# Another order of issue for the first 929 steps of a DeltaNet and MLP-mixer kernel

## The chip, the cores and the metric

The kernel runs on one core of one Trainium2 chip. The metric is the device time of one execution in microseconds, as the median of several runs. Besides TensorE (PE in the profile, with its weight loads as PEld) the core has VectorE (DVE), ScalarE (ACT), GpSimd (POOL) and SyncE (SP), which issues the DMA transfers. Each engine works through its own instructions in their order and waits on semaphores for the others.

## The reference

A linear recurrence of 8 heads with a 48 x 48 state each runs over 768 tokens for 4 batches. Its output, the heads side by side, goes through a token mixer and a channel mixer. Cut to what matters:

```python
B, H, S, D = 4, 8, 768, 48
k_n = k / (norm(k) + 1e-6)
for t in range(S):                       # per batch and head
    y[t] = q[t] @ state
    v_old = k_n[t] @ state
    state = state + beta[t] * outer(k_n[t], v[t] - v_old)
x = y.transpose(0, 2, 1, 3).reshape(B, S, H * D)          # [4, 768, 384]
h = relu(x.transpose(0, 2, 1) @ w_tok1) @ w_tok2          # 768 -> 256 -> 768
u = x + h.transpose(0, 2, 1)
out = u + relu(u @ w_ch1) @ w_ch2                         # 384 -> 1536 -> 384
```

## The kernel before

The recurrence is worked in chunks of 64 tokens. Two chunks make a unit u of 128 tokens, and a batch has 6 units, so there are 24 units and 48 chunks. For each chunk the products of the keys with one another are made, and with them a triangular system whose inverse turns the recurrence within the chunk into matrix products. The mixer follows batch by batch.

The work is written as generators, which stop after each step (a handful of instructions). They stand in a dictionary `jobs` under short names:

- `k3` loads the keys and queries of unit 3 (SP; copies on ACT, L396). `p3` prepares it: squares on ACT (L465), their sums on DVE (L468), the norm on ACT (L473, L474) and DVE (L477, L478), masks (L499), transposes on PE (L488, L507) with their copies on ACT (L491, L511), scaled keys (L516).
- `c3` and `d3` are the products of its two chunks (PE L442), with the masked evacuation on DVE (L445).
- `t3` takes the diagonal blocks out for the inversion (L598 on ACT, L603 on DVE, L605 on POOL). From the second round on they go through DRAM (L612 writes `n_dram`, L659 reads it into `x`).
- `i0`, `i1`, `i2` are rounds of that inversion, a chain of steps on DVE (L657, then pairs L676 and L680, then L682 to L693). `i0` serves the first units, `i1` and `i2` later ones. `f`, `h` and `j` join the inverted blocks into the inverse of a chunk (PE L710, L725, L760, L773; ACT L622, L716, L731, L754, L778; DVE L629, L749).
- `v3` loads values. `r10` is the recurrence's step for chunk 10: PE L837, ACT L843, PE L813, DVE L820, PE L851 and L852, DVE L860, ACT L865.
- `m0` is the mixer of batch 0: PE L1009, ACT L1017, PE L1022, six additions on DVE (L1026), transposes (PE L1032, ACT L1036), products (PE L1089 and later lines).
- `w29` is one piece of the weights: SP loads it (L273), ACT splits it (L279, L280), DVE shifts a part (L282), POOL joins the parts (L286). The load buffers are three, so a load waits for POOL's work on the piece three earlier. Some pieces of the last weight also make differences on DVE (L301). `s` sums weights, `b` loads beta.
- `x`, `z` and `Y` are products that nobody reads (L227, L237), which keep TensorE active.

Nothing reorders these steps. A string lists them, and a loop takes one step for each name (a number behind a star repeats it):

```python
    for word in order.split():
        name, _, n = word.partition("*")
        for _ in range(int(n or 1)):
            next(jobs[name])
```

The string has 2740 steps, and the order of instructions on each engine, the DMA issues on SP among them, follows from it. Buffers are counted: two for the values, two and two banks of PSUM for preparation and recurrence, three for the mixer.

Of the kernel before, what the change touches and what calls it, by code (L numbers as in the profile page):

```python
# [23 lines left out]
def kernel(  # L24
# [149 lines left out]
    t11 = const.tile([128, NB, HB], FP32, name="t11")  # L174
# [18 lines left out]
    w1 = const.tile([128, NCH, DTOK], FP32, name="w1")  # L193
    w2 = const.tile([128, NDH, S], FP32, name="w2")
# [993 lines left out]
    p1 c1*3 k2*4 p2 d1 x d1*3 k3 t0 p2*2 w3 d1 p2*2 w13 p2*4 c2*2 d2 p2 p3*2 k4*3  # L1188
    d2 k4*2 w3 w13 k6 w3*2 t0 w13*2 c2*2 k6 d2 k6 w1 k6*2 p3 k6 c2 d2*2 p3 x p3*5
    c3 d3 k4 c3 t1*2 p4 d3 x w18 c3 t1 t2 w18*2 w8 d3 c3 d3 k5 v1*2 d3 p4*2 k5*2 t0  # L1190
    c3 t2*2 t3*2 k7 p4 w1 t3 i0 p6 i0 p6*2 p4*2 i0*7 k8 z p4*4 v1 c4 k8 w6 d4 w1
    c4*4 d4*2 w8 w6 i0*2 d4 z v0*2 i0*3 x k8 z*3 w1 i0*2 d4 x w17*3 t4 z h0*4 i0
    k5*2 h1*2 k8 h1*2 h0 h1 w17 z f0*3 h0 w8*2 p3 v1 h0 p5 f1*3 k8 h0*3 v1 v0 h0*2
    v0 h2*3 t4 h2 h0 z f2 h2 w0*2 j0 w11 j0 w6 j0*4 k5 h1*6 j0*3 h1*2 f2*2 j1 p5 t4
    v0 j0*2 w6 p5*6 h2 p5 r0 w14 h2*2 r0*4 h2*4 c5*4 k7 k9 h2 r0*2 p8 p5 j1 c5 j1*2
    r0 k7 r1*2 k7 k9 r1 k9 w0*2 r1 d5*3 r1 k9 w11*3 d5*2 j1 r1 w14 p6*2 w9 p8 v2 j1
    h3*2 t5 j2 r1 p6 h3*2 f3 r1 k9*2 h3 j1*2 w14 j1*3 k7 p6 t5*2 r1*2 r2*3 w9 r2 x
    j2*3 i1*2 w14 j2*2 p6 r2*2 w16 r2 p6 f3*2 h3 i1*4 k10 r2*2 h3 i1 h3 d6 h3 p6 r2
    r3*2 d6 r3 d6 r3 i1 v2 x i1 h3*4 r3 d6 v2*2 w16 c6*2 w9 c6*2 k10 d6 c6 p7 w16
    p7 r3 j3 j2*2 r3 p7 r3*2 j2*2 j3 w9 j3 r4*2 k7 v3 p7 r4*2 j2 r3 j3*2 v2 j3 w16  # L1200
    r4 k10 p7*2 w24 v3 r4*2 k10 i1*2 t6 i1 w5 p7*2 r4 w27 p7 j3*4 r4*2 d7 i1 r5 i1
    r5 i1 r5 j3 k8 v3*2 d7 r5*2 d7*3 k10 w5 c7*3 r5 w27 w5 v4 r5 w5 c7*2 r5 p8*3
    r5*2 r6*4 w24 v4 t7 i1 z p8*4 p9 v3 r6 h5 w27 h5 v4*2 h5*3 r6*2 w26 h4*2 t7 d8
    h4 w24 i1 h4*2 t7 d8*3 r6 w24 w27 t7 c8*4 t6*2 f4*3 d8 h4*3 p9 w26 p9 r6 r7 k10
    r7 r6 h4 p8 c8 w28 t6 h4*3 v4 r7*2 h4 w7 p9 r7 p9*2 r7 p9*2 r7*2 p9 c9 w26 w28
    j4 d9 c9 w26 k11 c9*2 f5 p10 w28*2 d9*3 r7 c9 r8*2 w7 t8*2 d9 r8*2 j4*2 p10 t8
    j4*2 w7 j4 p7 p10 t8 v5 m0 f5 p10 p9 f5 v5 j4*3 w4 w15 w4 r7 t9*2 w4 j4*2 t9*2
    h5 w15 z r8*2 h5*2 v5 h5 v5 r8*2 w27 w7 w4 w15 Y r8 r9*4 h5*3 r8 p10 h5 i2 j5*2
    r9*2 i2 w29 j5 p10*2 r9 j5 i2*3 j5 w29 w12 k11*2 k12 j5 r9 i2 k11 v7 m0 r9 w15
    r10 j5*2 i2 j5 w12 w29 r10*2 i2 w19 i2 r10 p10 m0 p10 w19 k11*2 r9 v5 w12*2 k12  # L1210
    d10*2 i2 w22 j5 d10 j5 r10*2 x i2 d10 i2 r10 w19 Y r10 i2*2 m0 w29 r10 w19 z
    w21 Y p11 k12 r11 r10 w31 Y i2 w22*2 r11*3 k12 i2*2 r11 i2 m0 r11 i2*2 w22 v7*2
    c10 w31 r11*2 c10*2 i2 k12*2 r11 m0 x i2*4 v7 k12 i2*4 x z w25 v6*2 m0 i2*2 v6
    k12*2 v6 k12 i2 f6 m0*2 c10 m0 f6*3 w25 m0 c10 m0 w21 w25*3 f7 m0*2 p11 w21*2
    w23 f7 m0*2 w27 d10 m0 p11 j6 v6 j6*4 p10 f7 w31*2 f7 w30 f8*3 p12 j6 j7 p12
    w29 w23 t10 w29 w23 f9 m0 w25 j7 p12 j7*4 f8 m0 p11*3 r12*3 p12 r12 f9 r12 w23
    j8*2 f9 w30 t10 w23 r12 j8*3 r12*2 r13*3 j8 v7 w30 r13*2 m0 r13*2 p11 w32 p12
    p11*2 r13 t10 w20 s*2 k12 w30 w20 k12 v8 c11 w32 d11 c11 d11 r13 r14 t10 d11
    w31 r13 k13 c11 r14 w20 c11 w20 w23 d11 c11 d11 p12*2 r14*3 k13 m0*3 v8 w32 r14
    w32 k13*2 d12 c12*2 d12 c12 d12 c12*2 k13 w25 d12*2 p12 w31 r14*4 k13*2 m0*2  # L1220
    w27 w23 k13 r15*2 w29 k13*2 r15 j9 p11 p13 r15*2 p13 m0 p13*2 k13 p13 k13 p13
    r15 p13 m0*3 v8 w33 v8 d13 c13 t12 d13 c13 d13 c13 d13 c13 t11 r15*2 p13 r15
    t11*2 d13 c13 m0*2 t11 w33 r16*2 t12 r16 f9 t12 k14 r16 k14 j9*2 k14*2 w33*2 v8
    r16 j9*3 k14*2 m0*2 k14*2 m0 t13 m0 r15 t13 w33 r16 w33 p14*2 j9*2 t12 r16*3
    w33 r16 w31 m0 r17 p14*2 t13 j9 r17*2 j9 r17 p14 r17 t13 i3*2 k14 i3 m0*2 r17
    k14 v10 k15*2 i3*3 p14 i3 m0 k14 m0 i3 k14 v10 p14 i3*3 m0*2 i3 m0 k15*2 m0 r17
    i3 r17 m0 r17 v9*2 m0*2 i3*7 m0*3 i3*7 r18*2 i3*2 k15 v9 d14 r18 v9 k15*6 v10
    v9 i3*2 r17 i3 r18*2 f10 p15 m0*9 j9 f10*2 m0*2 f11 r18*2 k15 c14 d14 c14 d14
    p15 c14 d14 v10 r18 d14 r18 m0*4 r18 p15 r19 c14 s j10 r19*3 s r19 p15*2 f10
    m0*2 v10 f11 m0 r19*2 j10 f11*2 j10*2 f12 f13 r19*2 j10 j11 k16*2 p14 m0 k16  # L1230
    r20 k16 r20 k16*2 c14 t14 r20*2 p15 f12*2 j10 r20 j11 k16 j11*3 m0 k16 p15
    k16*2 r19 m0 j11 m0 r20 m0 s r20*2 d15*2 v11 p16 c15 r20 j12 d15 p16 c15 t14
    d15 c15 v11*2 r21 v11 c15*2 r21 p16 k16 r21*3 d15 t15 m0*2 r20 r21 p16*2 r21
    p16 m0 r21*2 j12*2 k16 j12 f13 k17 r21 j12*2 p16 r22*4 m0*2 p15 v11 r22*3 p16
    m0 k17*2 r22 k17*2 s*3 k17 r22*2 c16 d16 t15 c16 d16 f12 d16*3 c16 t15 r23 c16
# [72 lines left out]
```

## Time and profile before

| | us |
|---|---|
| median of three runs | 645.19 (644.68, 645.19, 655.08) |
| the profiled execution | 644.78 |
| its span in the trace | 643.0 |
| TensorE busy | 614.6 |
| VectorE busy | 446.1 |
| ScalarE busy | 259.8 |
| GpSimd busy | 108.9 |

The span is the time from the first to the last instruction that the trace shows; the execution is 1.78 us longer. The mean clock that TensorE was granted is 0.989 of full speed. A row of the trace's timeline gives the start and the duration in us, the engine, the line, the operation, output and input with partitions x elements, how many instructions of the kind follow one another, and in brackets how long the engine had been idle before and what ended that.

### The profile page before, as it was taken

Reading aid. Unit: us, or ns where it says so; the run is one execution under the profiler, and the core shown is the slowest. Engines: PE = TensorE matmul, PEld = TensorE weight load, DVE = VectorE, ACT = ScalarE, POOL = GpSimd, SP = SyncE. Lnnn points to the kernel's source line nnn. Section 1 sums busy time; section 2 is a strip of 40 time slices with the busy share of each in tenths; the row PEclk is TensorE's granted clock in tenths of the full one; section 3 lists DMA queues with packets and bytes.
Section 4 is the critical chain, followed back from the end, with each engine's and each line's share of the span. In section 5 each row is a group of like instructions: output and inputs, shape, how many; then the busy total and the mean of one; then the engine's idle time right before and its main releaser. Section 6 shows DMA issues by size and latency. Waiting matters only on the chain. (4 is left out here: it accounts for less than half of the span.)

```text
span 643.0 us, 21493 instructions
## 1 busy us (share of the span) xinstructions
PE 614.6 (96%) x9136; PEld 533.5 (83%) x9136; DVE 446.1 (69%) x1132; ACT 259.8 (40%) x631; POOL 108.9 (17%) x147
## 2 busy tenths in 40 slices
PE   8589899999999999999999999999999999999997
PEld 5358776678888988869899999769999987999997
DVE  4986877978789656988858997685726253373643
ACT  7759787436503332134523332234325140232240
POOL 2446264144200222021200010010020000000000
PEclk9989999999999999999979999999999999999999
DMA  9766667545543454343442222203010000000000
GB/s 192 165 131 156 147 149 199 151 116 131 100 112 76 75 112 107 75 106 70 96 99 68 58 78 44 66 11 53 4 42 4 25 3 0 25 1 25 1 26 25
DMA packets 135776, 50.27 MB, mean 78 GB/s; under 512 B 114656, under 2 KB 130144, under 8 KB 135680
## 3 DMA queue, kind: packets, MB, share of 16 engines
q1 hardware_dynamic: 135680, 48.89, 34.4%
q8 instruction: 72, 1.18, 0.8%
q14 instruction: 24, 0.20, 0.1%
HBM read 39.42 MB, written 9.44 MB: 76 GB/s over the span
## 5 line engine op out<-in xcount | busy, mean ns | idle before, releaser
L1111 PE MATMUL p_o<-wc,r 128*128 128x192 f32 x720 | 128.0, 332 | 0.6 <-ACT u_t L1036 0.6
L1111 PEld LDWEIGHTS p_o<-wc,r 128*128 128x128 f32 x720 | 118.5, 192 | 2.6 <-ACT u_t L1036 1.1
L993 DVE TENSOR_TENSOR r<-r,p_r 128x512 f32<-128x512 f32 x90 | 59.5, 683 | 39.4 <-PE p_r L981 36.9
L1040 DVE TENSOR_TENSOR xb<-xb,p_o 128x192 f32<-128x192 f32 x84 | 29.3, 350 | 57.5 <-PE p_o L1111 57.3
L990 ACT COPY r<-p_r 128x512 f32<-128x512 f32 x54 | 31.3, 584 | 85.9 <-PE p_r L981 78.6
L680 DVE TENSOR_TENSOR x<-x,sub 128x84 f32<-128x84 f32 (+24 forms) x178 | 59.9, 337 | 6.1
L676 DVE TENSOR_TENSOR sub<-x 128x84 f32<-128x84 f32 (+24 forms) x178 | 57.4, 322 | 6.5 <-DMA x<-n_dram 2.3
L1089 PE MATMUL p_c<-u_t,wc 128*128 128x256 f32 x216 | 51.3, 387 | 1.3 <-ACT r L1098 0.7
L1111 PE MATMUL p_o<-wc,s 128*128 128x192 f32 x288 | 51.2, 330 | 0.3 <-DVE xb L1040 0.3
L1111 PEld LDWEIGHTS p_o<-wc,s 128*128 128x128 f32 x288 | 46.8, 190 | 1.2 <-DVE xb L1040 0.6
L1089 PEld LDWEIGHTS p_c<-u_t,wc 128*128 128x128 f32 x216 | 39.6, 190 | 7.4 <-ACT r L1098 1.1
L416 POOL TENSOR_TENSOR v_st<-v_st,nrm 128x384 f32<-128x384 f32 x24 | 20.4, 849 | 148.1 <-DMA v_st<-in_v_dram 66.2
L442 PE MATMUL p_g<-kq 48*64 48x128 f32 (+1 forms) x704 | 38.6, 291 | 6.0 <-ACT kq L511 6.0
L997 ACT ACTIVATE r<-r 128x512 f32<-128x512 f32 x54 | 33.8, 631 | 25.5 <-DVE r L993 25.1
L499 POOL TENSOR_TENSOR mb<-mask_c,cs 128x512 f32<-128x512 f32 x20 | 21.0, 1049 | 129.6 <-DVE cs L478 103.7
L865 ACT ACTIVATE xb<-p_y 64x192 f32<-64x192 f32 x96 | 31.1, 324 | 24.0 <-PE p_y L852 16.3
L981 PE MATMUL p_r<-u_t,wc 128*128 128x128 f32 x288 | 38.6, 277 | 0.0
L981 PE MATMUL p_r<-t_d,wc 128*128 128x128 f32 x288 | 37.6, 281 | 0.0
L843 ACT COPY w_t<-p_w 128x192 f32<-128x192 f32 x48 | 15.3, 318 | 53.2 <-PE p_w L837 52.0
L442 PEld LDWEIGHTS p_g<-kq 48*64 48x64 f32 (+1 forms) x704 | 27.7, 140 | 10.0 <-ACT kq L511 6.8
L981 PEld LDWEIGHTS p_r<-u_t,wc 128*128 128x128 f32 x288 | 35.3, 192 | 0.3
L981 PEld LDWEIGHTS p_r<-t_d,wc 128*128 128x128 f32 x288 | 34.1, 191 | 0.9
(176 smaller groups left out, 1245.3 us busy)
## 6 DMA issues: line engine op xcount, KB each, us to landing
d<-in_moe_w_ch_dram SPq DMA_DIRECT2D x24, 384.0 KB, 3.9
v_st<-in_v_dram SPq DMA_DIRECT2D x96, 48.0 KB, 2.7
out_dram<-xb SPq DMA_DIRECT2D x23, 192.0 KB, 1.9
kst<-in_k_dram SPq DMA_DIRECT2D x64, 48.0 KB, 2.8
n_dram<-gm SPq DMA_DIRECT2D x72, 32.0 KB, 2.1
pads<-in_k_dram SPq DMA_DIRECT2D x24, 96.0 KB, 2.7
pads<-in_q_dram SPq DMA_DIRECT2D x24, 96.0 KB, 2.9
gm<-w_dram SPq DMA_DIRECT2D x72, 32.0 KB, 2.4
```

The lines of the kernel that those rows point to most:

```text
L442: nc.tensor.matmul(p_g[PAR[i ^ cc], p], kqt[f, p, cc, 0], kqt[f, p, cc])
L499: scaler.tensor_tensor(out=mb, in0=mask_c[:, None, None, :].to_broadcast([128, NP, 2, C]), in1=cs[:, :, :, None].to_broadcast([128, NP, 2, ...
L676: nc.vector.tensor_tensor(out=tmp, in0=col.to_broadcast(dims), in1=row.to_broadcast(dims), op=ALU.mult,)
L680: nc.vector.tensor_tensor(out=new, in0=new, in1=tmp, op=ALU.add)
L865: nc.scalar.mul(y[:, :, D * i : D * i + D], p_y[PAR[1 - i]], 1.0 if c else -1.0)
L981: nc.tensor.matmul(p[:, i], pieces[i // width][:, at : at + 128], f[f"u{n}"], start=first and i == 0, stop=True, skip_group_check=True,)
L990: nc.scalar.copy(o, p)
L993: nc.vector.tensor_tensor(out=o, in0=o, in1=p, op=ALU.add if sign > 0 else ALU.subtract)
L997: nc.scalar.activation(o, o, ACTF.Relu)
L1040: nc.vector.tensor_tensor(out=xb[:, c, e], in0=xb[:, c, e], in1=p, op=ALU.add)
L1089: nc.tensor.matmul(p_c[:, k], piece_of(wc1, cb, f * 128)[:, f * 128 : (f + 1) * 128], u_t[:, cb], start=(cb == 0), stop=(cb == NCB - 1),)
L1111: nc.tensor.matmul(p, a[:, m], wc2[:, m, j], start=(start and i == 0), stop=(i == NM - 1), skip_group_check=True,)
```

## The change

Only the string is different. Its first 929 steps are put in another order; every step that stood in the old string is there as often as before. The last 1811 steps are the same in the same order. The two strings begin like this:

```diff
     order = """
-    w10 z w10*2 z k1 z b k0 k1*2 b z x k1*2 k3 k0 z k1 k0*2 p1*2 k0 w2 k0 p0*2 b p1
-    p0 w10 p0*7 p1*3 k3*2 w2 d0 w2 c0 k2*2 c0 w18 d0*3 k3 w2 c0*3 d0 k3 p1*3 c1*2
...
+    z*4 w10*3 k1 k0 w10 b k0 k1*5 p1*2 k0*3 k3 k0 b p0 w2 p1 k2 b v1 p0*4 x k2 k3
+    p1 p0*2 p1 k4 p0 k3 p0 w2 k3 v1 w3 z c0 d0 c0 d0 k3 p0 d0 c0*2 k4 p1 w2*2 c0
...
```

What it moves is seen on the engines. Lines are those of the profile; a name with a number is one buffer of the name.

First place, DVE ahead of `i0`: the sums of squares L468 of `p2` and `p3`, and around them the evacuations L445 of `d1` and `c1`. Before:

```order
L516 TENSOR_TENSOR wc_127<-kst_94,cs 128x8x48
L445 TENSOR_TENSOR wc_127<-p_g,mb 128x4x128
L468 TENSOR_REDUCE ksum<-ksq 128x8
L445 TENSOR_TENSOR wc_127<-p_g,mb 128x4x128
L477 RECIPROCAL ksum<-ksum 128x8
L478 TENSOR_TENSOR cs<-ksum,beta_st 128x8
L499 TENSOR_TENSOR mb<-mask_c,cs 128x512
```

In the new order:

```order
L516 TENSOR_TENSOR wc_127<-kst_94,cs 128x8x48
L468 TENSOR_REDUCE ksum<-ksq 128x8
L445 TENSOR_TENSOR wc_127<-p_g,mb 128x4x128
L603 COPY r_130<-wc_127 32x8x32
L477 RECIPROCAL ksum<-ksum 128x8
L478 TENSOR_TENSOR cs<-ksum,beta_st 128x8
L445 TENSOR_TENSOR wc_127<-p_g,mb 128x4x128
L468 TENSOR_REDUCE ksum<-ksq 128x8
L499 TENSOR_TENSOR mb<-mask_c,cs 128x512
```

The sum for `p2` now stands ahead of both evacuations of unit 1, and the copy L603 of `t0` and the sum for `p3` ahead of the mask.

Second place, ACT ahead of `r0`: L754 is the last copy of the join `j0`, after which the recurrence's first product (L837) has its inverse. L473, L474, L491 and L511 are of `p5`. Before:

```order
L778 COPY zst<-p_z 32x256 x2
L731 COPY wc_127<-p_x 16x8x16 x4
L754 COPY wc_127<-p_x 32x8x32 x2
L473 ACTIVATE nrm_103<-ksum 128x8
L474 ACTIVATE ksum<-nrm_103,eps 128x8
L491 COPY kq_98<-p_t 128x4x128
L511 COPY kq_98<-p_t 128x4x128
L843 COPY w_t<-p_w 128x192
```

In the new order:

```order
L778 COPY zst<-p_z 32x256 x2
L731 COPY wc_127<-p_x 16x8x16 x4
L473 ACTIVATE nrm_103<-ksum 128x8
L474 ACTIVATE ksum<-nrm_103,eps 128x8
L491 COPY kq_98<-p_t 128x4x128
L754 COPY wc_127<-p_x 32x8x32 x2
L511 COPY kq_98<-p_t 128x4x128
L731 COPY gm<-p_x 16x8x16 x3
L843 COPY w_t<-p_w 128x192
```

Three instructions of `p5` went ahead of the join's last copy, and three copies of the next join ahead of the recurrence's.

Third place, DVE at the end of `i2` (its last pairs L676 and L680, widths 84 to 30), with the additions of `m0` (L1026). Before:

```order
L676 TENSOR_TENSOR sub<-x 128x84
L680 TENSOR_TENSOR x<-x,sub 128x28x3
L1026 TENSOR_TENSOR xb<-xb,p_h 128x384
L676 TENSOR_TENSOR sub<-x 128x58
L680 TENSOR_TENSOR x<-x,sub 128x29x2
L676 TENSOR_TENSOR sub<-x 128x30
L680 TENSOR_TENSOR x<-x,sub 128x30
L682 MEMSET x 128x32
L1026 TENSOR_TENSOR xb<-xb,p_h 128x384 x4
L445 TENSOR_TENSOR gm<-p_g,mb 128x4x128
L1026 TENSOR_TENSOR xb<-xb,p_h 128x384
```

In the new order (the first of the six additions stands just ahead of the step of width 168):

```order
L1026 TENSOR_TENSOR xb<-xb,p_h 128x384
L676 TENSOR_TENSOR sub<-x 128x108
L680 TENSOR_TENSOR x<-x,sub 128x27x4
L676 TENSOR_TENSOR sub<-x 128x84
L680 TENSOR_TENSOR x<-x,sub 128x28x3
L1026 TENSOR_TENSOR xb<-xb,p_h 128x384
L676 TENSOR_TENSOR sub<-x 128x58
L680 TENSOR_TENSOR x<-x,sub 128x29x2
L676 TENSOR_TENSOR sub<-x 128x30
L680 TENSOR_TENSOR x<-x,sub 128x30
L682 MEMSET x 128x32
L1026 TENSOR_TENSOR xb<-xb,p_h 128x384 x3
```

Three of the additions now stand among the inversion's last steps and three behind it, and the evacuation L445 has gone behind them all.

Further moves in the same 929 steps: the loads of the first values (`v0`, `v1`) and of the queries of unit 5 stand earlier; the four pieces of keep-warm work `z` that were spread over the start now come first; the weight pieces `w29`, `w12`, `w19`, `w4` and `w17` have more work between their load and ACT's first use of it, while `w22`, `w23` and `w31` have less; the recurrence's steps `r10` and `r11` stand earlier within `i2`; and the products of `m0` up to its additions stand later.

More of the change, by code (lines that the diff above doesn't have):

```diff
@@ L1192 @@
[L1192 to L1235, printed above, removed]
@@ new lines @@
+    r6 w24 i1 t6 h5 p9 h4*2 r6 c8*2 r6 c8*2 h4 d8 f4 d8*2 f4*2 v4 p9 r6 c8 w26 w28
+    d8 w26 r7 w26 d8 r7 h4*3 r7*2 r6 r7 h4*3 w7 h4 p9 w27 r7 h4 p9*2 r7 p9 j4 r7
+    p9 t8 d9 r7 d9*2 t8 c9 w28 c9 t8 w28 d9 w4 d9 v4 c9 r8*2 w28 p10 r8 t8 w7 c9
+    v5 j4 f5 j4 p8 j4 r8 c9 v5 j4*2 p10 f5 m0 j4 r7 j4 f5 j4 p10 j4 h5 w7 h5*2 j4
+    r8 w4 h5 w15 h5 p10 t9 w7 r8 z t9 h5 r8 w4 r8 w15 p9 t9*2 w27 p10 h5 k10 r8 r9
+    w15 r9 r8 v5*2 h5 r9*2 i2 w29 k11*2 j5*2 r9 j5 w4 k11 j5 p10 r9 j5 i2 v6 r9 j5
+    p10*2 w15 r9 j5*4 w12 r9 k12 k11 r10 i2 r10*2 p10 j5 r9 i2 v5 r10 w29 k11 m0
@@ new lines @@
+    r10 i2*3 w19 r10*3 w29 d10*2 i2 Y r10 r11 i2 r10 r11*2 w12 r11*4 c10 r11 x Y z
+    Y i2*2 r11 i2 k12*6 Y v7*2 p11 v7 w12 i2 k12 v6 p11 c10 i2 v7 p11 x i2 x c10
+    w19 p12 m0 w12 z w22 w29 i2*2 w19 v6*2 k12 i2*2 w22 i2*2 w19 w21 c10 w22 i2
+    k12 w22 d10 w25 i2*2 m0*4 i2 w21 w31 i2*2 m0 i2*2 m0 w25 i2*3 m0*2 w31 m0*4
+    w25*2 w29 w31 d10 w25 w21 d10 m0 w30 m0 p12 f6 v6 p12 f6 c10 f7 w29 m0 f6*2
+    w21 f7*2 w23 j6 f7 j6 f8 j6*3 f8 p10 j7 j6 j7*2 w23*2 f8 j7*2 w25 f9 w31 t10
+    j7 f8 m0 p11*3 r12*3 p12 r12 f9 r12 w23 j8*2 f9 w30 t10 w23 r12 j8*3 r12*2
@@ new lines @@
+    r13*3 j8 v7 w30 r13*2 m0 r13*2 p11 w32 p12 p11*2 r13 t10 w20 s*2 k12 w30 w20
+    k12 v8 c11 w32 d11 c11 d11 r13 r14 t10 d11 w31 r13 k13 c11 r14 w20 c11 w20 w23
+    d11 c11 d11 p12*2 r14*3 k13 m0*3 v8 w32 r14 w32 k13*2 d12 c12*2 d12 c12 d12
+    c12*2 k13 w25 d12*2 p12 w31 r14*4 k13*2 m0*2 w27 w23 k13 r15*2 w29 k13*2 r15
+    j9 p11 p13 r15*2 p13 m0 p13*2 k13 p13 k13 p13 r15 p13 m0*3 v8 w33 v8 d13 c13
+    t12 d13 c13 d13 c13 d13 c13 t11 r15*2 p13 r15 t11*2 d13 c13 m0*2 t11 w33 r16*2
+    t12 r16 f9 t12 k14 r16 k14 j9*2 k14*2 w33*2 v8 r16 j9*3 k14*2 m0*2 k14*2 m0
@@ new lines @@
+    t13 m0 r15 t13 w33 r16 w33 p14*2 j9*2 t12 r16*3 w33 r16 w31 m0 r17 p14*2 t13
+    j9 r17*2 j9 r17 p14 r17 t13 i3*2 k14 i3 m0*2 r17 k14 v10 k15*2 i3*3 p14 i3 m0
+    k14 m0 i3 k14 v10 p14 i3*3 m0*2 i3 m0 k15*2 m0 r17 i3 r17 m0 r17 v9*2 m0*2
+    i3*7 m0*3 i3*7 r18*2 i3*2 k15 v9 d14 r18 v9 k15*6 v10 v9 i3*2 r17 i3 r18*2 f10
+    p15 m0*9 j9 f10*2 m0*2 f11 r18*2 k15 c14 d14 c14 d14 p15 c14 d14 v10 r18 d14
+    r18 m0*4 r18 p15 r19 c14 s j10 r19*3 s r19 p15*2 f10 m0*2 v10 f11 m0 r19*2 j10
+    f11*2 j10*2 f12 f13 r19*2 j10 j11 k16*2 p14 m0 k16 r20 k16 r20 k16*2 c14 t14
@@ new lines @@
+    k20 s p19*2 d19*2 c19 s*2 f17 k20*2 d19 k20 c19 k20 d19*2 r28*4 k20*2 m1*2
+    p20*3 v15*2 c19 r29*2 c19*2 r29 v15 r29*2 m1*3 r29*2 p20 k20 p20 m1*2 r29 m1
+    j16 m1*2 r29*2 m1 k20*2 p20*2 v15*2 m1*4 r30 t18 j16*2 k21*4 m1*2 k21*8 r30*4
+    f17 t19 m1 j16 t19 j16*2 m1*2 r30 c20 p21*2 c20 d20 v16*3 c20 r30 c20*2 p21
+    t19 d20 r30 d20*2 r30 r31 p21 r30 d20 r31*4 p21 r31*2 p20 f17 m1 t20*2 m1 r31
+    p21*2 r31 c21 m1 j17 c21 d21 c21 t20 d21*2 t20 c21*2 d21 r32 f16 r32 t18*2 r32
+    d21 m1*9 r32 t21*3 j17 t21 t19 v16*2 i5 j17 v17*2 j17*2 f17 m1*2 k22*3 m1
```

82 lines of the change are left out of this document (47 added, 35 removed).

## The prediction

> **What bounds the kernel now.** I read the page's head first, then the busy time cut into five stretches, then TensorE's waits in the first four of them, and last the rows of each engine around the places where the two orders differ.
>
> ```profile
> span 643.0 us, 21493 instructions
> PE 614.6 (96%) x9136; PEld 533.5 (83%) x9136; DVE 446.1 (69%) x1132; ACT 259.8 (40%) x631; POOL 108.9 (17%) x147
> core 0: us, PE busy (x) PEld busy (x) DVE busy (x) ACT busy (x) POOL busy (x), PEclk, DMA share, GB/s
> 0.00:28.40 28.40, 21.38 (x232) 13.61 (x232) 19.19 (x54) 23.34 (x59) 9.75 (x20) 1.00 0.97 175
> 28.40:52.20 23.80, 18.32 (x294) 12.60 (x295) 19.73 (x49) 13.97 (x37) 13.11 (x16) 0.86 0.63 140
> 52.20:104.20 52.00, 46.66 (x1440) 39.83 (x1438) 39.31 (x101) 42.84 (x119) 29.23 (x36) 1.00 0.71 160
> 104.20:143.00 38.80, 36.09 (x483) 24.66 (x475) 33.09 (x93) 17.70 (x43) 9.21 (x11) 1.00 0.60 151
> 143.00:643.00 500.00, 492.17 (x6708) 442.77 (x6706) 334.75 (x836) 161.95 (x375) 47.59 (x65) 0.99 0.25 55
> ```
>
> A row of the second kind gives the stretch, its length, and the busy time of each engine. The last stretch is what the unchanged steps fill: TensorE is busy 492.2 of 500 us. The changed steps end near 143 us, which I call the joint. Behind it TensorE never has room to catch up, so a shift at the joint goes to the end one to one. Ahead of it TensorE idles 7.0 + 5.5 + 5.3 + 2.7 = 20.5 us. That is all a better order could win there, and no term below may exceed it.
>
> The same rows say what limits each of the four stretches. Up to 28.4 us ACT is busy 23.3 of 28.4. Up to 52.2 DVE is busy 19.7 of 23.8, with the first inversion i0. Up to 104.2 ACT (42.8 of 52) and DVE (39.3) are both loaded, but neither is full: 9.2 and 12.7 us are free. Up to 143 DVE is busy 33.1 of 38.8, with the third inversion i2.
>
> ```profile
> PE p_g L442 <- ACT kq L511: 6.0, 4, 3.5
> PE p_t L507 <- DMA pads<-in_q_dram: 2.8, 2, 2.5
> PE p_y L852 <- issue: 0.7, 2, 0.5
> PE p_k L813 <- issue: 0.6, 1, 0.6
> PE p_x L725 <- issue: 0.3, 1, 0.3
> ```
>
> These are TensorE's waits in 0 to 143 us (total, count, longest). The two large ones are for the prepared keys, while i0 is running on DVE. The rows with "issue", where nothing else that the profile shows was waited for, make 1.6 us together.
>
> **The change part by part.** Nothing is added or removed: the first 929 steps are the same steps in another order. So the sum has only shifts, at three places.
>
> *Place one, the start of i0.* In the new order DVE meets the sum of squares of p2 (L468) ahead of both evacuations of unit 1 (L445) that followed or preceded it, and has a copy of t0 (L603) between them.
>
> ```profile
> 15.86 0.69 DVE L445 TENSOR_TENSOR wc<-p_g,mb 128x512 f32<-128x512 f32 x1 [0.16 <-PE p_g L442]
> 16.71 0.55 DVE L468 TENSOR_REDUCE ksum<-ksq 128x8 f32<-128x384 f32 x1 [0.16 <-ACT ksq L465]
> 18.20 0.20 DVE L477 RECIPROCAL ksum<-ksum 128x8 f32<-128x8 f32 x1 [0.34 <-ACT ksum L474]
> 28.41 1.25 DVE L657 STREAM_TRANSPOSE x<-r 128x1024 f32<-128x1024 f32 x1
> ```
>
> (Columns: start, duration, engine, line, operation; in brackets the idle time before it and what ended it.) The evacuation L445 began at 15.86 and filled the time until ACT's squares were there at 16.71. ACT has the same 24 rows up to these squares in both orders, so they will not come earlier. Now DVE stands still from 15.86 to 16.71: 0.85 us. Against it, up to 0.16 + 0.34 = 0.5 us of idle time that stood here before can vanish, since the work that was moved behind now fills it; or the 0.34 stays as well. So i0 starts 0.35 to 1.2 us later; I take 0.85, or L657 at about 29.3.
>
> *Place two, the start of r0.* Ahead of the last join copy (L754, which frees the first inverse for r0) ACT now has the norm and the copy of p5.
>
> ```profile
> 51.41 0.75 ACT L754 COPY wc<-p_x 32x256 f32<-32x256 f32 x2
> 52.19 0.21 ACT L473 ACTIVATE nrm<-ksum 128x8 f32<-128x8 f32 x1
> 52.43 0.30 ACT L474 ACTIVATE ksum<-nrm,eps 128x8 f32<-128x8 f32 x1
> 52.76 0.58 ACT L491 COPY kq<-p_t 128x512 f32<-128x512 f32 x1
> ```
>
> That is 0.21 + 0.30 + 0.58 = 1.09 us on the way, if the chain through the joins sets the time; nothing, if ACT's queue sets it, because about as much work has left that queue further up. I take the middle, 0.55. With place one r0 is 1.4 us later, between 0.35 and 2.3.
>
> I cost this at nothing for the end. The cover is the free time of the third stretch, 12.7 us on DVE and 9.2 on ACT: the weight pieces w0 and p6.3 and p8.1, which stood between r1 and r2, now stand elsewhere, and r3 to r7 follow more closely. If that cover is gone, the price is the 1.4 to 2.3 us, and late next is the stretch's last product, the DMA hand-over to i2.
>
> *The start of i2* follows from the evacuations of c9 and d9 and a trip through DRAM.
>
> ```profile
> 94.05 1.29 DVE L445 TENSOR_TENSOR gm<-p_g,mb 128x512 f32<-128x512 f32 x2
> 104.25 0.19 DVE L676 TENSOR_TENSOR sub<-x 128x30 f32<-128x30 f32 x1 [0.89 <-DMA x<-n_dram]
> ```
>
> From the evacuations' end at 95.34 to i2's first step are 8.9 us of which little is DVE's. The two evacuations have changed places, and as much DVE work stands before them, so I leave i2's start at 104.2. What r4 to r7 gain is not on this way: the stores wait for both evacuations.
>
> *Place three, the end of i2 and the first mixer.* The six additions of mixer 0 (L1026) were one before and five behind the last steps of i2; now three stand before and three behind.
>
> ```profile
> 125.75 0.33 DVE L676 TENSOR_TENSOR sub<-x 128x168 f32<-128x168 f32 x1
> 128.90 0.55 DVE L1026 TENSOR_TENSOR xb<-xb,p_h 128x384 f32<-128x384 f32 x1
> 130.10 0.21 DVE L680 TENSOR_TENSOR x<-x,sub 128x30 f32<-128x30 f32 x1
> 132.77 0.56 DVE L1026 TENSOR_TENSOR xb<-xb,p_h 128x384 f32<-128x384 f32 x1 [0.74 <-PE p_h L1022]
> 134.13 0.55 DVE L1026 TENSOR_TENSOR xb<-xb,p_h 128x384 f32<-128x384 f32 x1 [0.20 <-PE p_h L1022]
> 134.39 0.86 ACT L1036 COPY u_t<-p_ut 128x384 f32<-128x384 f32 x2 [7.61 <-PE p_ut L1032]
> 142.98 1.56 PE L1089 MATMUL p_c<-u_t,wc 128*128 128x256 f32 x6
> ```
>
> The first addition moves ahead of the step of width 168, which began at 125.75. That saves 128.90 - 125.75 = 3.15 us, less one more L468 that now stands ahead of it (0.46 from start to start): near 126.2, if its product is there. The inversion's end moves back by two additions and the L468, 0.46 each from start to start, to 130.31 + 3 x 0.46 = 131.7. Three additions then end at about 133.1 if their products are ready, 134.7 if TensorE spaces them 1.36 apart as in the last two rows (134.13 - 132.77). The old end is 134.68. So the gain is between 0 and 1.6; I take the middle, 0.8. It cannot exceed the 2.7 us that TensorE idles in this stretch.
>
> In the same stretch r10 and r11 move far ahead, because ACT no longer waits on weight loads that it meets right after their issue:
>
> ```profile
> 106.86 0.57 ACT L279 ACTIVATE d<-d 128x384 f32<-128x384 f32 x1 [2.03 <-DMA d<-in_moe_w_ch_dram]
> 119.99 0.56 ACT L279 ACTIVATE d<-d 128x384 f32<-128x384 f32 x1 [2.85 <-DMA d<-in_moe_w_ch_dram]
> ```
>
> Those 2.03 + 2.85 = 4.9 us held the copies of the recurrence (L843) that are queued behind them. I cost this gain at nothing: TensorE is busy 36.1 of 38.8 us there, and the mixer's additions still wait for DVE's inversion.
>
> Last, the DVE and POOL hinder each other:
>
> ```profile
> 117.30 0.40 DVE L676 TENSOR_TENSOR sub<-x 128x240 f32<-128x240 f32 x1
> 117.73 1.10 DVE L680 TENSOR_TENSOR x<-x,sub 128x240 f32<-128x240 f32 x1
> 117.52 1.05 POOL L286 TENSOR_TENSOR wc<-w_f,d 128x384 uint32<-128x384 uint32 x1 [2.56 <-DVE w_f L282]
> ```
>
> An inversion step of 0.40 takes 1.10 while POOL joins a weight piece: 0.7 us a piece. DVE prepares four pieces (L282) ahead of the first addition in both orders, so the sum has zero; one more or one less on an inversion step is 0.7 either way.
>
> The sum: 644.78 of the profiled execution (span 643.0 and 1.78 around it), less 0.8, is 643.98. The median of the runs, 645.19, stands 0.41 above that execution. Forecast: **644.4**. Its own range, from the bounds at place three and 0.7 for one piece, is 642.4 to 646.4.
>
> On the packets in the change's name:
>
> ```profile
> q8 instruction: 19, 0.31, 1.0%
> 30.00:32.00 2.00, 0.00 (x0) 0.00 (x0) 1.83 (x8) 0.91 (x4) 0.29 (x1) 0.50 0.71 110
> 32.00:34.00 2.00, 1.39 (x22) 1.39 (x26) 1.79 (x7) 1.45 (x4) 0.00 (x0) 0.50 1.18 197
> ```
>
> The first row is the queue that fetches instructions, in the first 143 us: 19 packets, 1.0% of the DMA engines' time. By the Trainium skill ("Runtime: NRT & Kernel Launch", section "Instruction fetch mechanics") the sequencer fetches blocks of 16 KiB by itself, and crossing into the next one is "mostly hidden". 0.31 MB over 19 packets agrees with that size, and the 1.6 us of issue waits with "mostly"; by that rule heeding packets brings nothing, the forecast as it stands.
>
> The other two rows show the clock (third figure from the end) at half after TensorE stood idle. The Trainium skill ("TensorE: Matmul & The Clock Gate", section "What's actually happening") puts the halving behind an idle window of about 3.4 us. This case's wait of 3.5 us in this place agrees. It speaks against a later i0: an order with one more such hole would pay for it, as the first rival's upper end does.
>
> **The rivals.** (1) *Slower: the late start is not made good.* Place: L657, then r0. It decides if L657 starts after about 29.2 us and r0's first product is as far or farther behind 52.2. For it: ACT 82% and DVE 76% busy behind r0 are loaded queues, not free ones, and each is in order. Against it: 12.7 us free on DVE. Price: the upper 2.3 us, and no gain at place three because i2 then starts late as well: 644.78 + 2.3 + 0.41 = 647.5. With another 2 us stretch of half clock (1.4 busy at 0.50 is 0.7 lost) and pieces on the inversion, some 649.
>
> (2) *Faster: the middle's lead reaches i2.* The recurrence steps r4 to r7 stand 0.5 to 1.5 us ahead by the order. If the c9 evacuations come forward as much, and one idle wait of 0.89 before i2 goes, i2 starts 2.4 us earlier: 644.4 - 2.4 = 642.0. Its best case is half of DVE's 12.7 free us: 638.
>
> (3) *The packets matter.* The issue waits of 1.6 us in TensorE's rows go: 644.4 - 1.6 = 642.8. Against it: the order in front of a packet says nothing of when it is fetched, and 1.0% is little. That the change does nothing at all would be 645.2.
>
> (4) *Much slower*: a load whose use follows it too closely, as w22's, w23's and w31's now do, with two waits like the 2.85 above on the joint's path and the late start besides: 645.2 + 5.7 + 2.3 = 653.2.
>
> **How the numbers follow.** Forecast 0.42, rival 1 0.25, rival 2 0.15, rival 3 or no change 0.08, rival 4 0.10. I reach for 8 in 10 down to 639, near rival 2's best, and up to 652, short of rival 4. A measurement of this kernel can tell about 2% from no change, 12.9 us; below 632.3 lies nothing that the 20.5 us of idle time make likely, and above 658.1 only a rival 4 with a third or fourth such wait: faster 0.02, within 0.93, slower 0.05.
>
> **What would show it.** In the changed profile: L657 near 29.3 and the first p_w (L837) near 53.6; i2's first L676 near 104.2; no ACT wait over 2 us on L279 between 104 and 121; the first L1026 near 126.2, the last ending near 133.9; the six products of L1089 that start at 142.98 then start near 142.2; behind them the same 500 us. The prediction is wrong if TensorE's idle time up to the joint is not 20.5 - 0.8 = 19.7, if the stretch behind the joint changes by over 1 us, or if i2 starts more than 1.5 us off.

## The result: 0.6% slower, and the profile after

The changed kernel takes 648.61 us (median of 7 runs, 645.53 to 652.32), the kernel before in the same runs 644.68 us. The ratio is 1.0062, with a 95% interval of 1.0033 to 1.0091. In a second measurement (h2_ctrl below) it was 1.0076 (1.0051 to 1.0100). So the change costs about 4 to 5 us. That is inside 2%, but above the forecast of 644.4 with its own range to 646.4, and on the other side of no change. In the means further down, an execution more than 1.5% above the fastest of its kernel is left out.

Head of the changed kernel's page, whose profiled run took 647.93 us:

```profile
span 646.2 us, 21508 instructions
PE 616.6 (95%) x9136; PEld 533.8 (83%) x9136; DVE 443.8 (69%) x1132; ACT 260.8 (40%) x631; POOL 108.6 (17%) x147
```

TensorE does the same 9136 products, but is busy 2.0 us longer (616.6 against 614.6). Its idle time grew by 1.2 us only. The same products took longer, and the mean clock is lower (0.986 against 0.989).

The rows of the timeline that answer to those of the prediction, DVE, then ACT, then PE and SP:

```profile
16.46 0.55 DVE L468 TENSOR_REDUCE ksum<-ksq 128x8 f32<-128x384 f32 x1 [1.11 <-ACT ksq L465]
28.05 1.25 DVE L657 STREAM_TRANSPOSE x<-r 128x1024 f32<-128x1024 f32 x1
31.36 0.55 DVE L468 TENSOR_REDUCE ksum<-ksq 128x8 f32<-128x384 f32 x1 [1.50 <-ACT ksq L465]
107.91 0.19 DVE L676 TENSOR_TENSOR sub<-x 128x30 f32<-128x30 f32 x1 [3.02 <-DMA x<-n_dram]
130.67 0.55 DVE L1026 TENSOR_TENSOR xb<-xb,p_h 128x384 f32<-128x384 f32 x1
136.00 0.09 DVE L682 MEMSET x<- 128x32 f32 x1
136.41 1.06 DVE L1026 TENSOR_TENSOR xb<-xb,p_h 128x384 f32<-128x384 f32 x2
30.80 0.52 ACT L465 ACTIVATE ksq<-lent 128x384 f32<-128x384 f32 x1 [3.87 <-DMA lent<-in_k_dram]
53.10 0.21 ACT L473 ACTIVATE nrm<-ksum 128x8 f32<-128x8 f32 x1
54.15 0.75 ACT L754 COPY wc<-p_x 32x256 f32<-32x256 f32 x2
149.84 0.75 ACT L754 COPY gm<-p_x 32x256 f32<-32x256 f32 x2
54.73 0.88 PE L837 MATMUL p_w<-v_st,wc 64*64 64x48 f32 x16
102.25 0.46 SPq L659 DMA_DIRECT2D x<-n_dram  x1
```

And four rows of before that the prediction did not show:

```profile
130.29 0.09 DVE L682 MEMSET x<- 128x32 f32 x1
52.22 0.30 PE L837 MATMUL p_w<-v_st,wc 64*64 64x48 f32 x4
100.84 0.34 SPq L659 DMA_DIRECT2D x<-n_dram  x1
144.19 0.75 ACT L754 COPY gm<-p_x 32x256 f32<-32x256 f32 x2
```

Read in order of time, the lateness grows in steps along one chain. i0 starts 0.36 us *earlier* (28.05 against 28.41). But ACT then waits 3.87 us for the keys of unit 6, whose loads now stand behind four value loads on SP and are issued from 23.72 us on instead of 18.68. DVE stands 1.50 us inside i0 for the squares behind that wait. r0's first product is 2.5 us late (54.73 against 52.22). x for i2 is issued 1.4 us late and is used 5.7 us after its issue instead of 3.4, so i2 starts 3.7 us late. i2 takes 28.1 us from first step to L682 instead of 26.0. The join copy that frees r12 (L754) is 5.65 us late.

The windows show what came with it. First the changed kernel, then the kernel before around 320 us:

```profile
72.00:76.00 4.00, 2.49 (x101) 2.27 (x94) 3.25 (x13) 2.17 (x7) 1.01 (x1) 0.92 0.51 84
76.00:80.00 4.00, 4.00 (x89) 3.35 (x87) 2.27 (x8) 2.21 (x6) 1.99 (x3) 0.65 0.73 194
144.00:148.00 4.00, 2.48 (x75) 2.19 (x77) 1.05 (x4) 2.33 (x5) 0.11 (x1) 0.88 0.73 158
148.00:152.00 4.00, 4.00 (x62) 3.37 (x59) 3.09 (x8) 1.79 (x5) 3.04 (x4) 0.69 0.58 131
```

```profile
320.00:322.00 2.00, 1.07 (x23) 0.83 (x26) 1.44 (x6) 0.50 (x2) 0.96 (x1) 1.00 0.24 41
326.00:328.00 2.00, 2.00 (x20) 1.91 (x15) 1.82 (x6) 0.00 (x0) 0.00 (x0) 0.50 0.35 56
```

Twice in the changed kernel TensorE is busy only 2.5 of 4 us, and in the next 4 us its clock is 0.65 and 0.69. (In each row TensorE's busy time stands behind the length, and its clock is the third figure from the end.) In the profiled run before, TensorE's clock is full from 44 to 166 us, but there is such a stretch at 323 to 330, after 1.07 busy of 2. This stretch, of 6.8 us at half clock, fits that the two spans differ by 3.2 us only, though the joint is 5.65 us late.

Windows up to the joint give the sizes. Up to there TensorE does 2430 products in either kernel, 126.96 us busy of 148.65 in the changed one (mean clock 0.95) and 122.43 of 142.98 before (0.98). So 4.5 of the 5.7 us are longer products and 1.1 us are idle time. Behind the joint the sign turns, with 489.6 busy against 492.2.

There is also a longer hole in the front, while i0 runs on DVE:

```profile
33.46 1.97 PE L442 MATMUL p_g<-kq 64*64 64x128 f32 x16 [7.91 <-ACT kq L511]
```

TensorE waits 7.9 us at one go, where the kernel before waits 2.5 and 3.5 us with 0.6 us of work between. By windows of 1 us its clock is half from 27.6 to 37.8 us, before from 29.9 to 36.7. Much of that falls in the waits themselves, where a low clock costs nothing.

### The profile page after: what moved, and what is told of

Read it like the earlier page. It is cut to its first block, busy times and chain, and to the rows that moved or that the text cites. A ratio compares the mean times of both kernels' runs of the same rounds, so it can differ in the third digit from the quotient of the medians.

```text
span 646.2 us, 21508 instructions
## 1 busy us (share of the span) xinstructions
PE 616.6 (95%) x9136; PEld 533.8 (83%) x9136; DVE 443.8 (69%) x1132; ACT 260.8 (40%) x631; POOL 108.6 (17%) x147
## 5 line engine op out<-in xcount | busy, mean ns | idle before, releaser
L1111 PE MATMUL p_o<-wc,r 128*128 128x192 f32 x720 | 126.0, 329 | 0.6 <-ACT u_t L1036 0.6
L1111 PEld LDWEIGHTS p_o<-wc,r 128*128 128x128 f32 x720 | 116.7, 190 | 2.4 <-ACT u_t L1036 1.1
L993 DVE TENSOR_TENSOR r<-r,p_r 128x512 f32<-128x512 f32 x90 | 59.6, 684 | 39.7 <-PE p_r L981 39.0
L1040 DVE TENSOR_TENSOR xb<-xb,p_o 128x192 f32<-128x192 f32 x84 | 29.3, 350 | 53.8 <-PE p_o L1111 53.6
L680 DVE TENSOR_TENSOR x<-x,sub 128x84 f32<-128x84 f32 (+24 forms) x178 | 60.8, 342 | 6.1
L676 DVE TENSOR_TENSOR sub<-x 128x84 f32<-128x84 f32 (+24 forms) x178 | 58.6, 329 | 8.2 <-DMA x<-n_dram 4.4
L442 PE MATMUL p_g<-kq 48*64 48x128 f32 (+1 forms) x704 | 38.2, 281 | 12.5 <-ACT kq L511 11.0
L286 POOL TENSOR_TENSOR wc<-w_f,d 128x384 uint32<-128x384 uint32 x24 | 24.6, 1030 | 64.1 <-DVE w_f L282 31.2
```

The lines of the kernel that those rows point to most:

```text
L286: nc.gpsimd.tensor_tensor(out=dst.bitcast(U32), in0=f, in1=lo, op=ALU.add)
L442: nc.tensor.matmul(p_g[PAR[i ^ cc], p], kqt[f, p, cc, 0], kqt[f, p, cc])
L676: nc.vector.tensor_tensor(out=tmp, in0=col.to_broadcast(dims), in1=row.to_broadcast(dims), op=ALU.mult,)
L680: nc.vector.tensor_tensor(out=new, in0=new, in1=tmp, op=ALU.add)
L993: nc.vector.tensor_tensor(out=o, in0=o, in1=p, op=ALU.add if sign > 0 else ALU.subtract)
L1040: nc.vector.tensor_tensor(out=xb[:, c, e], in0=xb[:, c, e], in1=p, op=ALU.add)
```

## Experiments

Each kernel is the one or the other order with steps moved; `rest(s)` is the order s without the steps already done. Two theories stand against each other: the **chain** (late front, late x, longer i2) and the **clock** (holes in TensorE's work, half clock behind them).

### The order in parts

```diff
# e1_front_new
+order = new[:"r0"] + rest(old)
# e2_front_old
+order = old[:"r0"] + rest(new)
# e3_tail_new
+order = old[:"i2" second step] + rest(new)
# e4_tail_old
+order = new[:"i2" second step] + rest(old)
```

> The new order up to the first step of r0, then the old order (steps already done left out). Theory: the changed kernel is late in three portions on one chain: r0's first product 2.5 us late (54.73 against 52.22), i2's first step 3.7 us late (107.91 against 104.25), i2's end 5.7 us late (136.00 against 130.29), and the joint follows i2's end. By it the front alone makes r0 2.5 us late (54.7) and about 1.5 to 2 us of that reach i2's first step (106) and i2's end (132); time 644.7 + 2 = 646.7. Rival (the prediction's cover): the free time behind r0 takes it up, i2's first step at 104.2, time as before.

Measured: 647.29 us, ratio 1.0022 (0.9987 to 1.0057). r0's product at 53.98, i2's first step 107.15, its end 133.17.

> The old order up to the first step of r0, then the new order. Theory of three portions: r0 at 52.2, but the load of x for i2 still lands later because value and query loads are issued just ahead of it (5.6 us from issue to landing against 3.4), so i2's first step near 106.4, and i2 itself 2 us longer (28.1 against 26.0), its end near 134.5, 4.2 us late; time 648.9. Rival (the front is the whole cause): i2's first step near 104.2, time as before, 644.7.

Measured: 647.10 us, 1.0025 (0.9994 to 1.0056). r0 at 52.76, i2 from 104.86 to 132.22.

> The old order up to the second step of i2, then the new order. Theory: i2's first step at 104.2, i2 takes 28 us instead of 26, because two more additions of mixer 0 and one more sum of squares stand inside it, so its end is 2 us late (132.3) and the time 646.7. Rival (the prediction's place three): the additions that stand earlier let the mixer end 0.8 us earlier, and the joint with them; time 643.9.

Measured: 650.63 us, 1.0125 (1.0068 to 1.0183). i2 from 106.29 to 136.80: 30.5 us.

> The new order up to the second step of i2, then the old order. Theory: r0 at 54.7 and i2's first step near 107.9 as in the changed kernel, i2 26 us long, its end at 134, 3.7 us late; time 648.4. Rival (the lateness comes from the last third): i2's end near 130.3 and time as before, 644.7.

Measured: 649.38 us, 1.0082 (1.0036 to 1.0129). i2 from 113.25 to 139.29: 26.0 us.

What follows: neither e1 nor e2 is told from no change, while e3 and e4 are slower, and e3 by more than the whole change. The parts do not add up. i2 took 26.0 us in all three kernels with the old tail (before, e1, e4) and 27.4 to 30.5 in those with the new one, so the longer i2 belongs to the new tail: the theory's direction there is right, place three of the prediction wrong. But e3 went beyond the 646.7 of either theory, and its i2 start was at 106.29 although all its steps up to there are those of before (104.25). e4 missed by more: its steps up to i2 are those of the changed kernel, and yet i2 started at 113.25 instead of 107.91. Something that the order does not fix moves by 2 to 5 us from one execution to the next, so a difference of that size between two single traces says little. In e3's trace the clock was 0.84 between 70 and 80 us, in e4's it was half from 91 to 98.

### Setting single places right

```diff
# f2_front (in the new order)
-... p6 ahead of i0 ... p5*4 ahead of j0's last step
+... p6 behind p4's copies ... j0's last step ahead of p5
# f3_load
-k10's last step ahead of i2
+k10's last step behind i2's first step
# f1_adds
-m0 (2nd, 3rd addition) ahead of i2's end
+m0 (2nd, 3rd addition) behind i2's end
# g1_middle: old up to r0, new up to i2's second step with f3's edit, then old
```

> The changed order, but p6's squares (L465) come on ACT behind p4's copies and not ahead of them, and the last copy of join j0 (L754) comes ahead of p5's norm and copy. Theory: these two places made r0 2.5 us late (3.87 us of ACT's wait for the keys of unit 6, of which 1.5 reached i0, and 1.1 us of p5's work). Expected: no such wait of ACT, i0 from 28.1 to about 39.0, r0's first product near 52.7 instead of 54.73, i2's first step 1.5 to 2 us earlier than 107.9, time 646.8. Rival (r0's lateness does not matter behind it): r0 earlier, but i2's first step near 107.9 and time as the changed kernel, 648.6.

Measured: 649.15 us, 1.0047 (1.0010 to 1.0084). i0 from 28.40 to 39.12 (10.7 us, 12.1 in the changed kernel), r0 at 53.84 (52.7 was expected), i2's first step at 109.29. ACT's wait for the keys is gone, and i0 is as short as before the change (10.7). The wait does set i0's length: in the nine traces with the new front and p6 unmoved, i0 grows with it step by step, from 10.8 us at a wait of 2.56 (e1) to 12.5 at 4.31 (e4). r0 gained less, for e1 has it at 53.98 with no such edit.

> The changed order, but the load of queries of unit 10 (192 KB) is issued behind the load of x for i2 and not ahead of it. Theory: x lands 3.4 to 4 us after its issue instead of 5.6, i2's first step near 106, i2's end and the joint 1.7 to 2.2 us earlier, time 646.6. Rival (the landing is long for other reasons, such as the weight load and the three key loads issued behind it): still 5.6 us, time 648.6.

Measured: 651.47 us, 1.0066 (1.0034 to 1.0098). x issued at 102.93 and used at 108.47: still 5.5 us. The rival was right on the landing. On the time it was not: TensorE now waited 2.6 us for the moved queries themselves (until 109.51), the clock was half behind that, and i2 took 32.1 us.

> The changed order, but the second and third addition of mixer 0 stand behind i2's last step, as before the change. Theory: i2 takes 27.2 us instead of 28.1 (two additions of 0.46 fewer), the joint is 0.9 us earlier, time 647.7. Rival (prediction): the mixer's end sets the joint, so it comes later by 0.5 to 1 us, time 649.4.

Measured: 650.61 us, 1.0083 (1.0046 to 1.0121). i2 from 110.17 to 136.75, 26.6 us; the sixth addition ends 4 us behind i2. The two additions are worth some 0.7 to 1.5 us of i2 (27.3 us in h2_ctrl, 28.1 in the first profile), but the time didn't fall: the join copy L754 came 15.6 us behind i2's end (152.36), instead of 13.0 in h2_ctrl and 13.8 in the first profile.

> The old order up to r0, the new order from r0 to i2's second step, with the queries of unit 10 loaded behind the load of x, then the old order. Theory: the middle alone is better in the new order: x is issued near 99.2 (as where the old front was followed by the new rest) and lands 3.4 us later, i2's first step near 102.7, its end near 128.7, 1.6 us ahead of before; time 643. Rival (the middle gains nothing): i2's first step at 104.2, time 644.7 to 645.6.

Measured: 646.95 us, 0.9989 (0.9955 to 1.0023). i2's first step at 107.97; the forecast 643 was not reached.

None of the edits to the changed order brought the time back; g1, mostly the old order, is not told from before. In f2, f3, f1 and g1 there is a stretch of about half clock somewhere between 74 and 95 us, and in f3 and g1 a second one between 108 and 116. With these in the traces, the edits are not seen alone. f3's rows:

```profile
108.47 0.19 DVE L676 TENSOR_TENSOR sub<-x 128x30 f32<-128x30 f32 x1 [3.05 <-DMA x<-n_dram]
102.93 0.34 SPq L659 DMA_DIRECT2D x<-n_dram  x1
103.32 0.43 SPq L385 DMA_DIRECT2D lent<-in_q_dram  x1
```

### Filling the holes

```diff
# h1_warm (in the new order): six more z (128x512)
+z ahead of r3 ... +z behind r3's 4th and 6th step ... +z behind j6's 2nd, +z*2 behind its 5th step
# h2_ctrl: the new order, no edit
# h3_fix: the edits of f1 and f2, and
-loads of k10, k11, v6, w29 ahead of i2's third step
+loads of k10, k11, v6, w29 behind i2's third step
# h4_mid_warm (in g1_middle)
+z ahead of r3 ... +z behind r3's 4th step ... +z*2 ahead of r10
```

> The changed order with six more keep-warm products (128x512, about 0.53 us each) at the places where TensorE has holes: three around r3 (near 72 to 75 us) and three among the joins behind i2 (near 144 to 147 us). Theory of the clock: TensorE's holes there (busy 0.56 and 0.55 of 3.4 us) are what halves its clock in the two stretches behind them (74 to 79 and 146 to 151 us); filled, both stretches show a full clock, the profile's joint comes 1.5 to 3 us earlier, and the time is 646 to 647. Rival (the clock falls by chance or for other reasons): half-clock stretches there as often, and the time 0 to 3 us longer than the changed kernel's for the added products.

Measured: 647.49 us, 1.0009 (0.9992 to 1.0026), 645.9 to 649.1 in 11 runs.

> The changed order itself once more, on the same chip as the other three and with more rounds, as the measure for them: 0.3 to 0.9% slower than before, 647 to 651.

Measured: 651.95 us, 1.0076 (1.0051 to 1.0100), 648.4 to 654.8 in 8 runs.

> The changed order with all its suspected places set right: p6's squares behind p4's copies, the join's last copy ahead of p5, the loads of units 10 and 11 and of a weight piece behind i2's third step, and mixer 0's second and third addition behind i2's end. Theory of the chain (front, landing of x, length of i2): i2's first step near 104.5, its end near 131, time 645 to 646. Rival (these places do not carry the difference): time as the changed kernel's, 648 to 650.

Measured: 652.22 us, 1.0091 (1.0069 to 1.0112). Its moved loads change what some later products read, so its results are not the reference's and its time is a hint only. i2's first step at 109.56, not 104.5; clock 0.53 at 76 to 80 and 0.50 at 120 to 124. With f2_front's edits its i0 took 11.9 us all the same (DVE now waited 1.33 us for a product, L445), and r0 came at 55.22. Four places moved, nothing gained.

> The old order up to r0, the new one from r0 to i2's second step with unit 10's queries loaded behind x, the old order behind it, and four more keep-warm products: two around r3, two ahead of r10. Theory of the clock: without half-clock stretches between 70 and 116 us this is ahead of before: i2's first step near 103, time 642 to 644. Rival: as without the products, 645 to 647.

Measured: 647.62 us, 1.0016 (0.9991 to 1.0040), from 642.47 to 651.17; the fastest, the profiled one, has no half-clock stretch behind r0, and i2's first step at 105.23.

Six products that compute nothing took 4.5 us off the changed kernel (651.95 to 647.49, on one chip) and half of its spread (6.4 to 3.2 us). The same windows in h1_warm:

```profile
72.00:76.00 4.00, 3.48 (x110) 2.56 (x106) 1.99 (x6) 0.97 (x3) 1.01 (x1) 1.00 0.42 79
76.00:80.00 4.00, 4.00 (x130) 3.45 (x130) 3.73 (x14) 3.28 (x9) 1.72 (x2) 1.00 0.74 144
144.00:148.00 4.00, 4.00 (x67) 2.01 (x68) 1.40 (x5) 1.74 (x4) 0.49 (x1) 1.00 0.57 115
148.00:152.00 4.00, 3.98 (x113) 3.35 (x108) 3.06 (x6) 2.90 (x8) 2.51 (x4) 1.00 0.83 237
```

The holes are filled (3.48 and 4.00 busy where it was 2.49 and 2.48), and the clock behind them is full. In h2_ctrl, the control, they are there again, the first at another place:

```profile
88.00:92.00 4.00, 2.27 (x81) 2.15 (x79) 1.70 (x4) 1.56 (x7) 1.50 (x2) 0.77 0.40 64
92.00:96.00 4.00, 4.00 (x86) 4.00 (x84) 2.38 (x7) 2.58 (x7) 0.87 (x2) 0.50 0.51 188
148.00:152.00 4.00, 2.51 (x89) 2.21 (x86) 1.58 (x5) 2.27 (x6) 0.68 (x1) 0.95 0.69 153
152.00:156.00 4.00, 4.00 (x42) 3.04 (x40) 2.86 (x6) 1.95 (x6) 2.31 (x4) 0.63 0.61 152
```

This first hole of h2_ctrl ends with a wait of a kind that the profile doesn't explain:

```profile
91.36 0.53 PE L710 MATMUL p_z<-r,gm 64*64 64x32 f32 x5 [1.73 <-issue]
```

TensorE stood 1.73 us with nothing that the profile shows to wait for. Such waits of 1.2 to 2.0 us stand next to the half-clock stretch also in e3, e4, f1, f2, g1 and h3; e1 had one of 1.23 us and kept its clock. Between 44 and 166 us, h1, h4, j2 and j3 show none over 0.3 us. So the added products may have helped by covering these waits, and not only by holding the clock; no run separates the two, and what the waits are stays open.

### Which hole, and the other orders

```diff
# j3_warm_r3 (in the new order)
+z ahead of r3 ... +z behind r3's 4th and 6th step
# j4_warm_join (in the new order)
+z behind j6's 2nd, +z*2 behind its 5th step
# j1_before_warm (in the old order)
+z, five between r2 and r5 ... +z, three near r31
# j2_old_front_warm (in e2_front_old)
+z, the six of h1_warm
```

> The changed order with the three added keep-warm products around r3 alone. Theory of the clock: the hole near 72 to 75 us costs about half of the 4.3 us that all six brought (648.5 to 649.5 is left), and the stretch near 74 to 79 us shows a full clock, the one near 146 to 151 still half. Rival (one hole decides): this alone gives all, 647.5, or nothing, 650 to 652.

Measured: 647.44 us, 1.0001 (0.9970 to 1.0031). No half clock between 44 and 166 us, the stretch near 146 to 151 included, which was expected to stay. The rival was right: one hole gives all. The two holes' costs do not add up, for the next run recovers most of it at the other hole.

> The changed order with the three added products among the joins alone. Theory of the clock: the other half, 648.5 to 649.5, a full clock near 146 to 151 us and still half-clock stretches between 74 and 98. Rival: all or nothing, as for the products around r3.

Measured: 648.56 us, 1.0020 (0.9992 to 1.0048). Full clock around the joins, half at 66 and at 76 to 82. The forecast came true.

> The order before the change with eight added products at its own holes: five between r2 and r5 (65 to 80 us), three near 320 us. Theory of the clock: its executions too are spread by half-clock stretches (one lay at 322 to 330 us in its profile), so the median comes down to 643 to 644.5, and the spread shrinks. Rival (its spread has another cause): 646.5 and up to 4 us more for the products.

Measured: 649.51 us, 1.0053 (1.0022 to 1.0083). The rival was right: in the old order such products only cost.

> The old order up to r0, the new order behind it, with all six added products. Theory of front and clock together: the 2.5 us of the late front go, and the half-clock stretches too, so 644 to 645, ahead of before. Rival (the front does not carry through): as the changed order with the six products, 647.5.

Measured: 647.60 us, 0.9999 (0.9970 to 1.0028). Not ahead of before.

No version that I ran beats the kernel before beyond its interval.

Each run's mean granted clock gives an estimate of what the two theories are worth. Means over the executions of one call:

| kernel | us | clock | before in that call: us | clock |
|---|---|---|---|---|
| h2_ctrl (8) | 651.47 | 0.9839 | 646.39 (25) | 0.9895 |
| h1_warm (11) | 647.56 | 0.9940 | the same | |
| j3_warm_r3 (12) | 647.53 | 0.9906 | 646.93 (33) | 0.9890 |
| j4_warm_join (12) | 648.52 | 0.9888 | the same | |
| j2_old_front_warm (12) | 647.03 | 0.9929 | the same | |
| j1_before_warm (12) | 650.05 | 0.9896 | the same | |
| e1_front_new (10) | 647.24 | 0.9900 | 646.06 (20) | 0.9896 |

Among the executions of the kernel before, in each of the four calls, a clock lower by 0.001 went with 0.27 to 0.57 us more; I take 0.4. The changed kernel's clock is 0.0056 lower than before's: 2.2 of its 5.1 us, or 1.5 to 3.2 by the ends of that slope. The rest, 2.9, I put down to the chain. h1_warm agrees: its clock is 0.0045 above before's, worth 1.8, and yet it is 1.2 us slower, so at one clock 3.0. But this is no independent check, since six products of 0.53 us were added, and eight of them cost the old order 3.1 us at the same clock (j1). With the old front (j2) it is 1.6 + 0.1 = 1.7, so the front would carry about 1.3; e1_front_new, the front alone, gives 1.2 + 0.2 = 1.4. The interval of e1's 1.2 is some 2 us either way, so the front's share is not told from nothing.

What is shown is that added products at the holes take the half-clock stretches out of the changed order and 4.5 us off its time. The split between clock and chain is an estimate, and the chain's share is argued.

## Why the prediction was wrong

The step that failed and whose cost the runs show best is the clock: the sum has no term for it. Besides it, i2's start was held at 104.2, and place three was booked as a gain.

- *Clock*: I took one hole for both orders, because I looked for idle times of some 3.5 us. What the changed order has more of are stretches of low use: 2.5 busy of 4 us without one idle time over 1 us, and half clock behind them. Filling them took 4.5 us off (h1_warm against h2_ctrl). The Trainium skill ("TensorE: Matmul & The Clock Gate", section "What's actually happening") speaks of an idle window of about 3.4 us; these rows show that it need not be wholly idle. I also misread the hole in the front of the kernel before: its clock fell at 29.9 us, 0.8 us into the wait of 3.5 us and after 3.4 us with 0.6 us of work in them. That row was a thin stretch already. The upper end of rival 1 had one further such stretch at 0.7 us; by the mean clock, the changed order's cost 2.2 in all.
- *Bound and joint*: a shift at the joint goes to the end as far as the clock behind it is the same; in the profiles 2.4 of the 5.65 us came back, which fits before's own half-clock stretch at 323 (6.8 us at half, 3.4 us at most). TensorE's idle time up to the joint was 21.7 us, not the 19.7 that the prediction needed.
- *Place one*: wrong. DVE did stand still for p2's sum (1.11 us), but i0 started 0.36 us earlier, not 0.85 later; in all traces, with either front, it started between 27.8 and 28.6. The loss came inside i0, from ACT's 3.87 us wait for unit 6's keys. I had followed DVE and ACT, and left out where SP now had that load. The nine traces named at f2_front show it: wait and i0 grow together.
- *Place two*: the 0.55 for p5 ahead of L754 was too low. L754 starts 1.05 us after L473, with p5's three instructions between them, which is nearly the upper bound of 1.09. r0 was late by 2.5, my range ended at 2.3. In all traces r0 lies at 53.8 to 56.3 us with the new front and at 52.2 to 53.8 with the old one, so the direction holds.
- *The cover*: I cost r0's lateness at nothing because DVE and ACT have 12.7 and 9.2 us free behind it. In e1 the lateness of r0 (1.8 us) is followed by a late i2 (2.9 us), so the free time did not take it up in that trace. What of it reaches the end stays open: 1.3 to 1.4 us by estimate, within the noise. Rival 1 named this mechanism and 647.5, near the 648.6 measured, but that is in part luck: L657 did not start after 29.2, its point of decision, and by the estimate above more than half of the loss has other causes.
- *i2's start*: taken as unchanged, 3.7 us late in the first profile. The changed order unedited up to there gave 107.91, 108.21 (j4), 112.19 (h2_ctrl) and 113.25 (e4), the old one 104.25 and 106.29. That x is used later was not forecast: 3.9 to 5.7 us after its issue in the kernels with the new middle, 3.4 to 4.7 with the old one. f3 refuted the one load that I blamed, and the cause stays open; much of it changes from execution to execution.
- *Place three*: the first addition came at 130.67, not 126.2, for the most part i2's late start. More important, I let the mixer's end set the joint. In the first profile the joint moves with i2's end, through DRAM and the joins: i2 end 5.7 late, join copy 5.65 late, the sixth addition only 2.8 late. From i2's first step to that copy it is 39.7 to 40.0 us with the old tail (before, e1, e4, h4, j1) and 40.0 to 41.9 with the new one (the changed kernel, e2, f2, h2, j3): a cost of 0.1 to 2 us, where I had booked a gain of 0.8. It is not the two additions alone, for with them moved back (f1) it is 42.2.
- *The other rivals*: i2 did not start earlier (rival 2). ACT met no wait over 2 us on L279 between 104 and 121 us, as forecast; one of 2.79 us came at 124.18, and rival 4's pile of waits did not.
- *Packets*: "issue" stands for 1.6 us of TensorE's waits up to 143 us in both profiles, so it does not tell them apart. In other executions it stands for more (4.0 us up to 166 us in f1), in single waits of up to 2.0 us next to half-clock stretches. Whether these have to do with packets is not shown; that they are of no matter isn't either.
- *Median above the profiled run*: 0.41 was drawn from three runs; further runs of before spread from 641.8 to 653.7. The range of 642.4 to 646.4 is also half a us wider on each side than the bounds that it names (place three's 0 to 1.6 and 0.7 for a piece give 642.9 to 645.9). 648.61 lies outside both.

## What to carry to other kernels

Free time on the busy engines behind a late start is no proof of a cover: it has to lie on the chain from that start to the next meeting point. Follow that chain, its loads included, before costing the start at nothing. When reordering fills one engine better and leaves TensorE thinly used for some microseconds elsewhere, look at the granted clock behind those places, and measure with a few keep-warm products there: three at one hole recovered nearly all here, while eight in the old order cost 0.5%. Compare executions at their granted clock, since one profile may carry a low stretch that the other does not. And take several traces of one kernel before reading a difference of a few us off two of them.

## What the runs showed of the hardware

That TensorE's clock halves after a *thin* stretch, not only after an idle one, was new to me. It fell after 2.49 and 2.48 busy of 4 us in the changed kernel and after 1.07 of 2 us in the kernel before, with no single wait over 1 us. By windows of 1 us it stayed at half for about 3.4 us each time in the changed kernel, and for about 6.8 us in the kernel before. It does not fall each time: in e1_front_new a wait of 1.67 us, up to 110.22, was passed at full clock. And the same steps on the same data put i2's first step at 104.25 in one execution and 106.29 in another of the old order, and at 107.91, 112.19 and 113.25 in three of the new one.
